# Moving two small coefficient loads, one subtraction of three heads and one step of seven weight blocks in a fused attention and two-layer expert kernel

## The chip, the cores and the metric

The kernel runs on one core of a Trainium2 chip. The metric is the device time of one execution in microseconds (us); lower is better. Five engines work side by side, each through its own queue in order: PE (TensorE, matmuls, with its weight loads shown as PEld), DVE (VectorE), ACT (ScalarE), POOL (GpSimd) and SP (SyncE), which here only issues DMAs. They wait for one another by semaphores.

## The reference

Three stages, all in float32, one after the other:

```python
# attention: 4 batches x 8 heads, 576 positions, 64 channels, causal by blocks of 64
scores = scale * q @ k^T ;  mask where block(i) < block(j) ;  attn = softmax(scores) ;  x = attn @ v
# first layer:  2304 tokens, 512 -> 2048 -> 512
x = leaky_relu(x @ w_in) @ w_out            # slope 0.01
# second layer: 2304 tokens, 512 -> 2048 -> 512
h = x @ w_in ;  P = a0 + a1 h + a2 h^2 + a3 h^3 ;  Q = 1 + |b0||h| + |b1|h^2
out = (P / (Q + 1e-6)) @ w_out
```

The weights arrive as 64-bit numbers and are read as pairs of 32-bit words.

## The kernel before

**Precision.** A matmul operand that must be exact is kept as a rounded high part and the rest, its low part ("hi" and "lo"). A product is then the sum of three matmuls (high by high, and the two crosses), two for the scores of attention. Heads 0 to 7 (`NSF = 8`, `WHOLE = 8`) are computed with plain float32 operands. From head 8 on the heads are "split": `a1(n)` (L249 to L268) makes of q the tiles `QT` and `QM`, of k the tiles `KH` (high part, in both halves) and `KL`, whose upper half is the low part of k, k minus its high part (L266). In the trace these tiles bear the names `split_fq` and `split_fk`. Which engine makes which is told by the letters of `E1` (L124): p is POOL, v DVE, a ACT; the sixth letter is that of L266. The matmuls of scores that read them are L295.

**One head.** The scores go to PSUM (L289 for plain heads, L295 for split ones), DVE takes the row maximum (L301), ACT the exponential (L307), DVE sums and reciprocals (L313, L314), DVE for plain and POOL for split heads scales the probabilities (L317), PE transposes them (L344), ACT and DVE copy them to SBUF (L327 for plain heads; L329, L334, L337 for split ones), PE multiplies by v (L372, L376), and ACT and DVE write the head's result (L383 to L385 for plain heads, L389 to L394 for split ones). After the eighth head of a batch SP saves its last 64 positions (`save_left`, L403). The loop over the 32 heads (L702 to L745) runs these steps for three neighbouring heads at a time, in an order given by strings (`ORDER0`, `ORDER1`, `ORDER`).

**Filling.** When a batch of 8 heads is done, `moe1(b)`, the first layer for its tokens, becomes a filler: a fixed number of its matmuls (L461) is put between the steps of the next batch's heads (`fill`, `FILL`). The 32 units of a batch use the weight blocks one by one; a unit in which the low weights come from memory loads them on SP (L430), up to five units ahead. `gh`, `gl` (L469 to L471) are the activated results, `acc` (L476, L478) their sums.

**Weights.** Each of 64 blocks of weights goes through `convert()` (L157 to L188): SP loads 512 KB into `cs` (L147, three buffers), ACT makes the high words (L165), the low words are made by POOL for the blocks 0 to 15 (L169) and by ACT for all later ones (L171), DVE joins both (L180), ACT rounds (L183), POOL subtracts to get the low part (L184), SP writes it out (L154). Blocks 0 to 31 are the first layer's, the others the second's. How many steps of it stand between the steps of each head is a written list (`due`, `pace`, L675 to L689).

```python
165  nc.scalar.activation(hi.bitcast(F32), hi.bitcast(F32), AF.Prelu, ...)
168  if i < 16:
169      nc.gpsimd.tensor_scalar(lo, lo.bitcast(U32), 0.875 * 2.0 ** -29, 0.4375, ALU.mult, ALU.add)
170  else:
171      nc.scalar.activation(lo, lo.bitcast(U32), AF.Copy, scale=0.875 * 2.0 ** -29, bias=0.4375)
```

**Coefficients.** `cab` (a and b of the second layer, spread over 128 partitions) is loaded on SP near the start, after the first heads' loads (L668, L669); DVE negates a (L670), ACT takes the magnitude of b (L671). They are read only in the second layer (L575 to L589).

**The end.** After the last head the rest of the first layer runs in slices of 24 matmuls (L759 to L774), between which SP loads second-layer weights and the saved positions (L762), and ACT and DVE split them (L764, L765). Then comes the second layer (`moe2`: L563, L617).

**Order.** Only SP's order is the one written in the program (L651). On PE, DVE, ACT and POOL the framework's planner, which sorts ready instructions by priority and by estimated costs, sets the order, so that an instruction can run well ahead of or behind the place where it stands in the code; on the chip each queue then runs in that order.

Of the kernel before, what the change touches and what calls it, by code (L numbers as in the profile page):

```python
# [14 lines left out]
AF = mybir.ActivationFunctionType  # L15
ALU = mybir.AluOpType
# [9 lines left out]
def attention_moe_moe_kernel(  # L26
# [13 lines left out]
    nc = tc.nc  # L40
    P = 128
# [39 lines left out]
    cab = const.tile([P, 6], F32, name="cab")  # L81
    coef = const.tile([P, 6], F32, name="coef")
# [38 lines left out]
    W2H = dram.tile([NF, P, 2 * KD, P], F32, name="w2h")  # L121
    W2L = dram.tile([NF, P, 2 * KD, P], F32, name="w2l")
    NSF = 8
    E1 = "pvpapv"  # L124
    CUTS = [5, 9, 13, 16]
    blocks = []
    for g, c in enumerate(CUTS):
# [16 lines left out]
    def load_block(i):  # L144
        if i < len(blocks):
            stage[i] = cp.tile([P, 512, 2], I32, tag="cs", name="cs", bufs=3)
            nc.sync.dma_start(out=stage[i].rearrange("p (r n) w -> p r (n w)", r=KD), in_=blocks[i][0])  # L147
# [3 lines left out]
    def write_block():  # L151
        if split:
            for d, t in split.pop():
                nc.sync.dma_start(out=d, in_=t)  # L154
            ndone[0] += 1

    def convert():  # L157
        load_block(0)
        load_block(1)
        for i in range(len(blocks) + 1):  # L160
            if i > 0:
                load_block(i + 1)
            if i < len(blocks):
                hi, lo = stage[i][:, :, 1], stage[i][:, :, 0]
                nc.scalar.activation(  # L165
                    hi.bitcast(F32), hi.bitcast(F32), AF.Prelu, scale=2.0 ** -112, alpha=-(2.0 ** 32)
                )
                if i < 16:
                    nc.gpsimd.tensor_scalar(lo, lo.bitcast(U32), 0.875 * 2.0 ** -29, 0.4375, ALU.mult, ALU.add)  # L169
                else:  # L170
                    nc.scalar.activation(lo, lo.bitcast(U32), AF.Copy, scale=0.875 * 2.0 ** -29, bias=0.4375)  # L171
            if i > 0:
                s = stage.pop(i - 1)
                _, (dh, dl), kept = blocks[i - 1]
                hi, lo = s[:, :, 1], s[:, :, 0]
                f = cp.tile([P, KD, P], F32, tag="cl", name="cl", bufs=3)
                wh = dh if kept else cp.tile([P, KD, P], F32R, tag="ch", name="ch", bufs=2)
                hi, lo = (x.rearrange("p (r c) -> p r c", c=P) for x in (hi, lo))
                yield
                nc.vector.scalar_tensor_tensor(  # L180
                    f.bitcast(I32), hi, 3, lo, ALU.logical_shift_left, ALU.bitwise_or
                )
                nc.scalar.copy(wh, f)  # L183
                nc.gpsimd.tensor_tensor(f.bitcast(F32R), f, wh.bitcast(F32), ALU.subtract)  # L184
                write_block()
                split.append(((dh, wh.bitcast(F32)), (dl, f))[kept:])
                yield
        write_block()  # L188

    ndone = [0]  # L190
    conv = convert()

    def cv(n):
# [21 lines left out]
    def split_tiles(n):  # L215
        e, j = n % 2, (2 * n - NSF) % 4
        for d, nm, i in ((QT, "fq", j), (KH, "fk", j), (QM, "fq", j + 1), (KL, "fk", j + 1)):
            d[e] = ap.tile([P, S], F32R, tag=f"{nm}{i % 4}", name=f"split_{nm}{i % 4}")
        for c, d in enumerate((QM, KL)):
            src = plain[(NSF - 1) % 4][c] if n == NSF else d[1 - e].bitcast(F32)  # L220
            cp1("p", d[e][D:P, :], src[D:P, :])
# [19 lines left out]
    def cp1(eng, out, in_, by=1.0):  # L241
        if eng == "a":
            nc.scalar.activation(out, in_, AF.Copy, scale=by)
        elif eng == "v":
            nc.vector.tensor_scalar(out, in_, by, None, ALU.mult)
        else:
            nc.gpsimd.tensor_scalar(out, in_, by, 1.0, ALU.mult, ALU.mult)

    def a1(n):  # L249
        if n < NSF:  # L250
            if n > 0:
                fq = plain[n % 4][0][0:D, :]
                cp1("a", fq, fq, SCALE)
            return
        if n < NSF + 2:
            split_tiles(n)
        e = n % 2
        qs, ks = qk[e][0:D, :], qk[e][D:P, :]
        cp1(E1[0], QT[e][0:D, :], qs, SCALE)
        nc.vector.scalar_tensor_tensor(  # L260
            QT[e][D:P, :], qs, SCALE, QT[e][0:D, :].bitcast(F32), ALU.mult, ALU.subtract
        )
        cp1(E1[2], QM[e][0:D, :], QT[e][0:D, :].bitcast(F32))
        cp1(E1[3], KH[e][D:P, :], ks)
        cp1(E1[4], KH[e][0:D, :], ks)
        (nc.vector if E1[5] == "v" else nc.gpsimd).tensor_tensor(  # L266
            KL[e][0:D, :], ks, KH[e][D:P, :].bitcast(F32), ALU.subtract
        )  # L268

# [218 lines left out]
    def fill(n):  # L488
        if filler[0] is None:
            return  # L490
        for _ in range(n):
            if next(filler[0], 0) == 0:
                filler[0] = None
                return
# [17 lines left out]
    def load_w2_by_part(f, wh, wl):  # L512
        W2[f] = (wh, wl)
        for t, w in ((wh, W2H), (wl, W2L)):
            nc.sync.dma_start(out=t.bitcast(F32), in_=w[f].rearrange("p k c -> p (k c)"))
            yield
# [4 lines left out]
    def x_tiles():  # L521
        return tuple(xp.tile([P, KD, NT1], F32R, tag=nm, name=nm) for nm in ("xh", "xl"))

    def w2_in_x(pair, i):
        x = pair[i].rearrange("p k s -> p (k s)")
        return x[:, 0:1024], x[:, 1024:2048]
# [4 lines left out]
    def load_x2(c):  # L531
        t0, n = chunks[c]
        h = xq[c % 2].tile([P, KD, 512], F32R, tag="x2h", name="x2h")
        l = xq[c % 2].tile([P, KD, 512], F32R, tag="x2l", name="x2l")
        XC[c] = (h, l)
        for t, x in ((h, x2hd), (l, x2ld)):
            nc.sync.dma_start(
                out=t[:, :, 0:n].bitcast(F32), in_=x[:, t0:t0 + n].rearrange("(k p) t -> p k t", p=P)
            )
            yield  # L540
# [110 lines left out]
    with tc.manual_schedule(engines={mybir.EngineType.SP}):  # L651
# [13 lines left out]
            for i in range(5):  # L665
                nc.gpsimd.memset(PB[e][i][:, KEYS[i]:], 0.0)
        nc.vector.memset(cq, 1.0 + EPS_Q)
        nc.sync.dma_start(out=cab[:, 0:4], in_=ca.partition_broadcast(P))  # L668
        nc.sync.dma_start(out=cab[:, 4:6], in_=cb.partition_broadcast(P))  # L669
        nc.vector.tensor_scalar(coef[:, 0:4], cab[:, 0:4], -1.0, None, ALU.mult)  # L670
        nc.scalar.activation(coef[:, 4:6], cab[:, 4:6], AF.Abs)  # L671

        heads = [(b, h) for b in range(B) for h in range(H)]

# [27 lines left out]
        for n, (b, h) in enumerate(heads):  # L702
# [8 lines left out]
            for step, f in zip(steps, fills):  # L711
                if step == "1" and n + 1 < NHD:
                    a1(n + 1)
                elif step == "v":
                    if n >= WHOLE:
                        a1v(n)
                    if n < WHOLE and odd and 0 < p:
                        load_v(p + 1)
                elif step == "4":
                    save_left()  # L720
                    apply(n - 2)
                elif step == "x":
                    a2_part(n, [(0, 4)], (nm, sm))
                elif step == "y":
                    a2_part(n, [(0, 3), (512, 2)], (nm, sm))
                elif step == "z":
                    a2_part(n, [(0, 1), (512, 0)], (nm, sm))
                elif step == "a" and n > 0:
                    if n >= WHOLE and odd and p < NHD // 2 - 1:
                        load_v(p + 1)  # L730
                    a3a(n - 1)
                elif step == "b" and n > 0:
                    a3b(n - 1)
                if step == max("xyz", key=steps.index):
                    a2_norm(n, sm)
                fill(f)
                pace(n, steps.index(step) + 1)
# [21 lines left out]
        for i in range(32):  # L759
            fill(24)  # L760
            if i == 1:
                nc.sync.dma_start(out=X[B][1].bitcast(F32), in_=xld.rearrange("p k b t -> p k (b t)"))  # L762
            elif i == 14:
                nc.scalar.copy(X[B][0], X[B][1].bitcast(F32))  # L764
                nc.vector.tensor_tensor(X[B][1], X[B][1].bitcast(F32), X[B][0].bitcast(F32), ALU.subtract)  # L765
            elif i < 14:
                next(loads, None)
            elif i == 15:
                pair = x_tiles()
                loads = chain(*(load_w2_by_part(NA + 2 + f, *w2_in_x(pair, f)) for f in range(2)))  # L770
                loads = chain(loads, load_x2(0))
                filler[0] = moe1(B) if filler[0] is None else chain(filler[0], moe1(B))
            elif i % 2:
                next(loads, None)  # L774
# [45 lines left out]
```

## Time and profile before

| | |
|---|---|
| median of 3 runs | 1052.02 us (1050.37 to 1052.32) |
| profiled execution, its own time | 1049.87 us |
| its span in the trace | 1048.1 us |
| PE busy | 1000.8 us (95%) |
| DVE, ACT, POOL busy | 741.6, 665.6, 274.0 us (71%, 64%, 26%) |
| mean granted TensorE clock | 0.995 |

Up to about 500 us the 32 heads run, from about 82 us on with the first layer as filler; from there to 645 us the rest of the first layer, then the second. An engine's busy time says how much of the span it worked; the idle time in brackets of a timeline row says how long it stood before that instruction and which instruction of another engine ended the wait.

### The profile page before, as it was taken

The numbers are of one execution on the slowest core, as the hardware profiler recorded it, in microseconds if no ns is written. First come the engines' busy times: TensorE is split into PE (matmuls) and PEld (weight loads), VectorE is DVE, ScalarE is ACT, GpSimd is POOL, SyncE is SP. The second block draws the span as 40 slices with busy tenths as digits, with TensorE's granted clock in tenths as the row PEclk, the third lists the DMA queues.
The fourth block names the chain that finished last, engine by engine and source line by source line (L and its number), as shares of the span: only waits on it lengthen the run. The fifth ranks groups of instructions, "written<-read, shape, count | busy, mean of one in ns | idle before, by whom it ended". The sixth has DMA issues, their size and how long they took to land.

```text
span 1048.1 us, 14697 instructions
## 1 busy us (share of the span) xinstructions
PE 1000.8 (95%) x4968; PEld 826.2 (79%) x4968; DVE 741.6 (71%) x1273; ACT 665.6 (64%) x1364; POOL 274.0 (26%) x329
## 2 busy tenths in 40 slices
PE   7988888898999989999999999999999999999998
PEld 5656767787888877788888899888888888888886
DVE  4896777666777666766332223999888888888875
ACT  5776688776777766675321224876766666676675
POOL 3355656555554545453100101000000000000000
PEclk9999999999999999999999999999999999999999
DMA  8475868668577677564655587802102010110010
GB/s 204 139 208 177 274 191 277 194 211 267 193 229 208 212 249 227 167 221 132 203 192 183 195 286 280 331 1 81 41 1 81 1 40 1 41 41 1 1 41 21
DMA packets 101995, 158.32 MB, mean 151 GB/s; under 512 B 11168, under 2 KB 48032, under 8 KB 101920
## 3 DMA queue, kind: packets, MB, share of 16 engines
q1 hardware_dynamic: 101920, 157.39, 46.8%
q8 instruction: 39, 0.64, 0.2%
q14 instruction: 36, 0.29, 0.1%
HBM read 116.92 MB, written 39.85 MB: 150 GB/s over the span
## 4 chain that ended last, share of the span: by engine, by line
PE 66%; DMA 7%; ACT 5%; DVE 4%; issue 3%; POOL 1%; SPq 1%; ACTq 0%; DVEq 0%; POOLq 0%
PE M L461 23%; PE h L563 19%; PE o L617 19%; DMA cs<-in_moe_w_in_dram 3%; PE T L344 2%; PE T L295 1%; ACT PB L307 1%; PE T L376 1%; DMA cs<-in_moe_w_out_dram 1%; DMA vr<-in_v_dram 1%; ACT pTh L329 1%; ACT cs L165 1%; DMA xld<-vr 1%; DMA w2h<-ch 1%; DVE pTl L337 1%
## 5 line engine op out<-in xcount | busy, mean ns | idle before, releaser
L461 PE MATMUL M<-gh,w1o 128*128 128x512 f32 (+1 forms) x320 | 121.1, 378 | 6.4 <-DVE vr L390 2.5
L461 PE MATMUL M<-gl,w1o 128*128 128x512 f32 (+1 forms) x320 | 121.0, 378 | 0.0
L461 PE MATMUL M<-gh,wl 128*128 128x512 f32 (+1 forms) x320 | 120.5, 377 | 0.0
L575 ACT ACTIVATE ea<-h,coef 128x512 f32<-128x512 f32 (+1 forms) x80 | 51.6, 645 | 92.7 <-PE h L563 92.7
L307 ACT ACTIVATE PB<-T,nm 128x448 f32<-128x448 f32 (+4 forms) x160 | 82.8, 523 | 36.0 <-DVE nm L301 34.0
L469 ACT ACTIVATE gh<-M 128x512 fp32r<-128x512 f32 (+1 forms) x80 | 44.4, 555 | 89.5 <-PE M L461 89.4
L471 DVE TENSOR_TENSOR gl<-M,gh 128x512 fp32r<-128x512 f32 (+1 forms) x80 | 50.4, 632 | 65.5 <-ACT M L470 65.5
L563 PE MATMUL h<-x2h,w2l 128*128 128x512 f32 (+1 forms) x240 | 88.9, 370 | 0.0
L563 PE MATMUL h<-x2h,w2h 128*128 128x512 f32 (+1 forms) x240 | 88.8, 370 | 0.0
L563 PE MATMUL h<-x2l,w2h 128*128 128x512 f32 (+1 forms) x240 | 88.8, 370 | 0.0
L317 POOL TENSOR_SCALAR PB<-PB,sm 128x448 f32<-128x448 f32 (+4 forms) x120 | 71.5, 615 | 53.3 <-DVE sm L314 53.3
L617 PE MATMUL o<-w2h,g2l 128*128 128x512 f32 x216 | 84.7, 392 | 0.0
L617 PE MATMUL o<-w2h,g2h 128*128 128x512 f32 x216 | 84.7, 392 | 0.0
L617 PE MATMUL o<-w2l,g2h 128*128 128x512 f32 x216 | 84.6, 391 | 0.0
L461 PE MATMUL M<-xh,w1i 128*128 128x512 f32 x256 | 76.2, 407 | 5.4 <-DVE vr L390 4.4
L578 DVE SCALAR_TENSOR_TENSOR ea<-eh,coef,ea 128x512 f32<-128x512 f32 (+1 forms) x80 | 55.7, 696 | 34.9 <-ACT eh L576 34.3
L344 PE MATMUL T<-ident,PB 128*128 128x128 f32 x480 | 67.3, 280 | 13.3 <-ACT PB L307 8.8
L301 DVE TENSOR_REDUCE nm<-T 128x1 f32<-128x448 f32 (+4 forms) x160 | 71.7, 479 | 10.7 <-PE T L289 8.7
L344 PEld LDWEIGHTS T<-ident,PB 128*128 128x128 f32 x480 | 55.0, 143 | 28.1 <-ACT PB L307 10.9
L461 PE MATMUL M<-xl,w1i 128*128 128x512 f32 x256 | 72.4, 397 | 3.9 <-DVE xl L384 2.4
L180 DVE SCALAR_TENSOR_TENSOR cl<-cs 128x512 int32<-128x512 int32 x64 | 57.3, 898 | 24.9 <-ACT cs L171 8.3
L461 PEld LDWEIGHTS M<-gh,w1o 128*128 128x128 f32 x320 | 60.7, 190 | 17.6 <-DVE gl L471 2.9
(121 smaller groups left out, 2536.3 us busy)
## 6 DMA issues: line engine op xcount, KB each, us to landing
wl<-w1l SPq DMA_DIRECT2D x160, 256.0 KB, 3.2
cs<-in_moe_w_in_dram SPq DMA_DIRECT2D x32, 512.0 KB, 5.4
cs<-in_moe_w_out_dram SPq DMA_DIRECT2D x32, 512.0 KB, 5.5
w1l<-cl SPq DMA_DIRECT2D x32, 256.0 KB, 4.5
w2h<-ch SPq DMA_DIRECT2D x32, 256.0 KB, 3.6
w2l<-cl SPq DMA_DIRECT2D x32, 256.0 KB, 3.9
w2h<-w2h SPq DMA_DIRECT2D x12, 512.0 KB, 6.5
w2l<-w2l SPq DMA_DIRECT2D x12, 512.0 KB, 7.1
```

The costliest lines, as they stand in the source:

```text
L180: nc.vector.scalar_tensor_tensor(f.bitcast(I32), hi, 3, lo, ALU.logical_shift_left, ALU.bitwise_or)
L301: nc.vector.tensor_reduce(nm[:, i:i + 1], sc, axis=AX.X, op=ALU.max, negate=True)
L307: nc.scalar.activation(PB[e][i][:, 0:ln], sc, AF.Exp, scale=SCALE if n == 0 else 1.0, bias=nm[:, i:i + 1], accum_out=sm[:, i:i + 1])
L317: (nc.vector if n < WHOLE else nc.gpsimd).tensor_scalar(PB[e][i][:, 0:ln], PB[e][i][:, 0:ln], sm[:, i:i + 1], 1.0, ALU.mult, ALU.mult)
L344: nc.tensor.transpose(T[:, c:c + P], PB[e][i][:, kt * P:(kt + 1) * P], ident)
L461: nc.tensor.matmul(T, lhsT=w[:, kk, :], rhs=A[kk][lo], start=(m == 0), stop=(m == 11))
L469: nc.scalar.activation(gh, T, AF.Prelu, alpha=0.01)
L471: nc.vector.tensor_tensor(gl, T, gh.bitcast(F32), ALU.subtract)
L563: nc.tensor.matmul(h[:, 0:n], lhsT=a, rhs=x, start=(kk == 0 and i == 0), stop=(kk == KD - 1 and i == 2))
L575: nc.scalar.activation(a, h, AF.Abs, scale=coef[:, 4:5])
L578: nc.vector.scalar_tensor_tensor(a, h2, coef[:, 5:6], a, ALU.mult, ALU.add)
L617: nc.tensor.matmul(ob[t], lhsT=a, rhs=w, start=(f == 0 and i == 0), stop=(f == NF - 1 and i == 2))
```

## The change

The two loads of coefficients and their two small instructions go from the start to the last group of the first layer: the loads behind the load of the saved positions, the instructions behind the split of these. L266 goes from DVE to POOL for the heads 8, 9 and 10. The low words of the blocks 9 to 15 are made by ACT in place of POOL. The sixth letter of `E1` is not needed any more.

```diff
-    E1 = "pvpapv"
+    E1 = "pvpap"
...
-                if i < 16:
+                if i < 9:
                     nc.gpsimd.tensor_scalar(lo, lo.bitcast(U32), 0.875 * 2.0 ** -29, 0.4375, ALU.mult, ALU.add)
                 else:
                     nc.scalar.activation(lo, lo.bitcast(U32), AF.Copy, scale=0.875 * 2.0 ** -29, bias=0.4375)
...
-        (nc.vector if E1[5] == "v" else nc.gpsimd).tensor_tensor(
+        (nc.gpsimd if n < NSF + 3 else nc.vector).tensor_tensor(
             KL[e][0:D, :], ks, KH[e][D:P, :].bitcast(F32), ALU.subtract
         )
...
         nc.vector.memset(cq, 1.0 + EPS_Q)
-        nc.sync.dma_start(out=cab[:, 0:4], in_=ca.partition_broadcast(P))
-        nc.sync.dma_start(out=cab[:, 4:6], in_=cb.partition_broadcast(P))
-        nc.vector.tensor_scalar(coef[:, 0:4], cab[:, 0:4], -1.0, None, ALU.mult)
-        nc.scalar.activation(coef[:, 4:6], cab[:, 4:6], AF.Abs)
...
             if i == 1:
                 nc.sync.dma_start(out=X[B][1].bitcast(F32), in_=xld.rearrange("p k b t -> p k (b t)"))
+                nc.sync.dma_start(out=cab[:, 0:4], in_=ca.partition_broadcast(P))
+                nc.sync.dma_start(out=cab[:, 4:6], in_=cb.partition_broadcast(P))
             elif i == 14:
                 nc.scalar.copy(X[B][0], X[B][1].bitcast(F32))
                 nc.vector.tensor_tensor(X[B][1], X[B][1].bitcast(F32), X[B][0].bitcast(F32), ALU.subtract)
+                nc.vector.tensor_scalar(coef[:, 0:4], cab[:, 0:4], -1.0, None, ALU.mult)
+                nc.scalar.activation(coef[:, 4:6], cab[:, 4:6], AF.Abs)
```

## Rows read from the trace of the kernel before

**Rows 1.** The page, part 1: busy time, share of the span, instructions.

```profile
PE 1000.8 (95%) x4968; PEld 826.2 (79%) x4968; DVE 741.6 (71%) x1273; ACT 665.6 (64%) x1364; POOL 274.0 (26%) x329
```

**Rows 2.** Windows: busy time and count per engine, TensorE's granted clock, DMA share, GB/s.

```profile
60.00:80.00 20.00, 16.22 (x84) 11.23 (x82) 19.75 (x40) 14.29 (x37) 10.43 (x11) 1.00 0.62 194
80.00:100.00 20.00, 15.74 (x76) 11.95 (x74) 12.64 (x22) 12.46 (x28) 12.14 (x13) 0.91 0.38 115
100.00:120.00 20.00, 17.29 (x92) 14.29 (x91) 13.50 (x23) 14.49 (x32) 11.97 (x14) 1.00 1.02 334
...
500.00:550.00 50.00, 50.00 (x220) 40.67 (x219) 15.06 (x22) 14.58 (x25) 5.16 (x4) 1.00 0.62 206
```

**Rows 3.** Timeline, 12 to 20 us: start, duration, engine, line, idle before and releaser.

```profile
12.06 0.58 SPq L668 DMA_DIRECT2D cab<-in_moe_a_dram  x1
12.69 0.45 SPq L669 DMA_DIRECT2D cab<-in_moe_b_dram  x1
...
14.83 0.17 DVE L670 TENSOR_SCALAR coef<-cab 128x4 f32<-128x4 f32 x1 [1.25 <-DMA cab<-in_moe_a_dram]
...
15.96 0.30 PE L344 MATMUL T<-ident,PB 128*128 128x128 f32 x1 [3.27 <-DVE PB L317]
...
16.18 0.20 ACT L671 ACTIVATE coef<-cab 128x2 f32<-128x2 f32 x1 [2.61 <-DMA cab<-in_moe_b_dram]
...
19.46 0.66 POOL L169 TENSOR_SCALAR cs<-cs 128x512 int32<-128x512 uint32 x1 [13.51 <-DMA cs<-in_moe_w_in_dram]
```

**Rows 4.** L266, L171 and L184 by line: shortest, median and longest in ns.

```profile
L266 DVE TENSOR_TENSOR split_fk<-qk,split_fk x24: 753/755/3704, 61.8 to 460.0; 64x576 fp32r<-64x576 f32 x24
...
L171 ACT ACTIVATE cs<-cs x48: 643/668/738, 116.5 to 472.1; 128x512 int32<-128x512 uint32 x48
...
L184 POOL TENSOR_TENSOR cl<-cl,w1o x16: 1267/1282/1735, 47.8 to 197.3; 128x512 fp32r<-128x512 f32 x16
```

**Rows 5.** Timeline, 61 to 77 us.

```profile
61.76 1.11 DVE L266 TENSOR_TENSOR split_fk<-qk,split_fk 64x576 fp32r<-64x576 f32 x1
...
72.33 3.70 DVE L266 TENSOR_TENSOR split_fk<-qk,split_fk 64x576 fp32r<-64x576 f32 x1
...
74.16 1.27 POOL L184 TENSOR_TENSOR cl<-cl,w1i 128x512 fp32r<-128x512 f32 x1
...
76.63 2.10 PE L376 MATMUL T<-acc,vr 128*128 128x448 f32 x8 [2.02 <-DVE acc L327]
```

**Rows 6.** Timeline, 85 to 92 us.

```profile
85.91 3.49 POOL L317 TENSOR_SCALAR PB<-PB,sm 128x448 f32<-128x448 f32 x5
...
89.49 0.64 POOL L169 TENSOR_SCALAR cs<-cs 128x512 int32<-128x512 uint32 x1
90.16 0.69 DVE L180 SCALAR_TENSOR_TENSOR cl<-cs 128x512 int32<-128x512 int32 x1 [2.57 <-POOL cs L169]
...
91.63 0.50 PE L461 MATMUL M<-xl,w1i 128*128 128x512 f32 x1 [2.45 <-DVE xl L384]
...
91.75 0.61 SPq L403 DMA_DIRECT2D xld<-acc  x1
```

**Rows 7.** Timeline by engine, 112 to 117 us.

```profile
112.98 0.67 POOL L169 TENSOR_SCALAR cs<-cs 128x512 int32<-128x512 uint32 x1
...
113.68 0.69 DVE L180 SCALAR_TENSOR_TENSOR cl<-cs 128x512 int32<-128x512 int32 x1 [2.46 <-POOL cs L169]
...
116.79 0.50 PE L461 MATMUL M<-gh,w1o 128*128 128x512 f32 x1 [1.92 <-DVE gl L471]
```

**Rows 8.** Windows of 4 us: the same columns as in rows 2.

```profile
92.00:96.00 4.00, 4.00 (x14) 3.22 (x13) 1.53 (x3) 2.06 (x6) 1.22 (x1) 0.57 0.66 175
...
104.00:108.00 4.00, 4.00 (x23) 3.51 (x22) 3.90 (x8) 3.16 (x7) 2.72 (x4) 1.00 1.10 345
```

**Rows 9.** Timeline of ACT, 79 to 83 us: the exponentials behind L165 of two blocks.

```profile
79.95 0.64 ACT L307 ACTIVATE PB<-T,nm 128x448 f32<-128x448 f32 x1 [0.24 <-DVE nm L301]
...
82.49 0.42 ACT L307 ACTIVATE PB<-T,nm 128x192 f32<-128x192 f32 x1
```

## The prediction

> **What bounds the kernel now.** I began with the busy times: TensorE works 1000.8 of 1048.1 us [rows 1], so a change that leaves its work alone, as this one does, can win at most the other 47 us, and only where TensorE stands idle or runs at half its clock. The windows say where that is. From 500 us on TensorE is never idle (50.00 of 50.00) and DVE and ACT are 30% busy [rows 2]: nothing moved there counts. Between 60 and 120 us it is idle for 3.78, 4.26 and 2.71 us, 10.75 in all, and in the first of these slices DVE is busy 19.75 of 20 us [rows 2]: there DVE is the bound, and TensorE waits for it. So I read that stretch in the timeline, engine by engine, and the first 20 us, where the coefficients are. Every edit but the move into the last group falls in these two places.
>
> **Part 1, the coefficients leave the start.** DVE stood 1.25 us for the first load and then took 0.17, ACT stood 2.61 and took 0.20; TensorE's transposes stood 3.27 us for the normalised probabilities that DVE makes behind its coefficient instruction [rows 3]. SP's two issues end about 1.1 us after the first begins [rows 3]. At most 1.25 + 0.17 = 1.42 us come free on TensorE's path. But behind it ACT meets the first weight block's first instruction, whose data POOL was still waiting for at 19.46 [rows 3]: that landing moves only as far as SP's issues do, 1.1 us at most, less because the next load waits for the tiles of head 0. Bounds 0 and 1.42; I take 0.5, nearer to the landing, because that wait ends last. In the last group the loads stand behind the load of the saved positions: two SP issues of 0.58 and 0.45, ahead of weight loads that are five units early, and 0.17 + 0.20 us on DVE and ACT while these are 30% busy and TensorE never idle [rows 2, 3]. What hides them is that idle time; if the two instructions were put ahead of their data, DVE and ACT would stand as at the start, at most 2.61 us, with four score banks and five early units of cover. Cost 0.
>
> **Part 2, L266 of heads 8, 9 and 10 goes to GpSimd.** A clean L266 costs DVE 0.755 us (median); of the three that move, head 8's took 1.11 and head 9's 3.70; head 10's I put at no more than head 8's and count it at nothing here [rows 4, 5]. The long one is not work: it began at 72.33 and ended at 76.03, 0.6 us after GpSimd's subtraction that began at 74.16 and took 1.27 had ended [rows 5]. DVE stood for GpSimd's two-input instructions, one behind the other, and TensorE stood 2.02 us at 76.63 for the PSUM copy queued behind L266 on DVE [rows 5]. On GpSimd the operation isn't in the trace. The nearest row is L184, the same subtraction with 512 elements per partition: 1.28 us [rows 4]; at 576 that scales to 1.44. From below 0.755, as on DVE; I take 1.4. So GpSimd gets 3 x 1.4 = 4.2 us more. It gives up 7 low-word steps of 0.64 to 0.67 us [rows 6, 7], 4.6 us, and is busy 10 to 12 of 20 us [rows 2]. The product KL is needed only when the head's scores run, several us later, so its own lateness costs nothing.
> - Head 8: DVE is full, so its 1.11 us come back: 1.1 (0 to 1.1).
> - Head 9: the PSUM copy moves up to 72.3 and TensorE's 2.02 us go. Next late are the sums (L313) and the scaling (L317) of head 7, which came behind L266's end at 76.03 and may now stand for GpSimd in its turn. 2.0 (0 to 3.7).
> - What the new GpSimd instructions hold up on DVE: bounds 0 and 4.2; I take one of the three in full, 1.4, since only at head 9 is GpSimd's queue packed.
>
> **Part 3, the low words of blocks 9 to 15 go to ACT.** Each takes 0.668 us on ACT (median of L171), 7 x 0.668 = 4.7 us in all [rows 4], in a stretch where ACT is busy 14.3, 12.5 and 14.5 of 20 us [rows 2]. What it frees is a queue, not work.
> - Block 12: GpSimd's L169 stood behind the five scalings (85.91, 3.49 us); DVE's join of the words stood 2.57 us for it, with the writing of head 7's result behind it on DVE. For that TensorE stood 2.45 us at 91.63, and SP, whose saving of the last positions (L403) it also holds, issued nothing until 91.75 [rows 6]. ACT has the word ready right behind L165. TensorE's 2.45 us go (0 to 2.45). Head 10's L266, which was ahead of that join, is gone as well.
> - The clock: after that idle time TensorE had a stretch at the lower level, the mean of the slice from 92 is 0.57 [rows 8]. At about 0.5 for 3.4 us it costs 1.7 us. If the idle time goes, I expect the stretch to go, but the low weights, loaded only after L403, then come in second: 0.85 (0 to 1.7).
> - Block 15: the same pattern, DVE stood 2.46 us behind GpSimd and TensorE 1.92 us for `gl` [rows 7]: 1.9 (0 to 2.4).
> - The price on ACT: where an exponential stands right behind L165, it comes 0.668 us later. That is so for blocks 10 and 11, with ACT idle 0.24 us or not at all before it [rows 9]: 2 x 0.668 = 1.35. Bounds 0 and 4.7.
>
> **The sum.** 0.5 + 1.1 + 2.0 - 1.4 + 2.45 + 0.85 + 1.9 - 1.35 = 6.05 us. Against the profiled execution's own 1049.87 us (span 1048.1 and 1.8 around it) that gives 1043.8. This execution was 2.15 us below the median shown, 1052.02; the runs lie 2 us apart. From the median: 1052.02 - 6.05 = 1046.0. A measurement of this kernel can tell about 0.2%, 2.1 us, from no change, so under 1049.9 is faster and over 1054.1 slower.
>
> **Rivals.**
> 1. The wait only changes sides. GpSimd's run at 72.3 gets 1.4 us longer and DVE's sums of head 7 stand for its end at about 76.8 (75.43 + 1.4), where they came behind 76.03: head 9 brings 0, head 8 0.4, block 12 gives back 1.4, and the half-clock stretch stays. 0.5 + 0.4 + 0 + (2.45 - 1.4) + 1.9 - 1.35 = 2.5 us, 1049.5. For it: L266 got no turn in 3.1 us between GpSimd's instructions [rows 5]. Against it: only at head 9 do they stand so close, and the PSUM copy needs no turn. The Trainium skill, SBUF — State Buffer, section "SBUF: two separate sides", says the same of the hardware: DVE and GpSimd share a pair of ports as an exclusive lock, held for a whole instruction, and a DVE instruction with two SBUF inputs stands until GpSimd's is done. The 3.70 us of L266 agree. By that rule alone each of the three would cost DVE up to 1.4 where it saved 0.755. Chance 0.2.
> 2. The transfers take over. From 100 us on the DMA engines are full (share 1.02, and 1.10 in the slice from 104) [rows 2, 8]. If what was won before 92 us is lost waiting for weights, about 1.5 us are left: 1050.5. For it: those slices. Against it: the full stretch begins when SP gets past L403, which comes earlier too. Chance 0.14.
> 3. Slower: ACT becomes the bound between 60 and 120 us. All seven steps lie ahead of something that is waited for, 4.7 us, and the freed waits turn into waits for ACT, of which only the 2.0 us of head 9 stay won: 1052.0 + 4.7 - 2.0 = 1054.7. It decides if of ACT's 18.8 idle us between 60 and 120 [rows 2] hardly any lies where a step is put. Against it: at blocks 12 and 15 ACT was idle, waiting for DVE's join. Chance 0.08.
> 4. Larger: the half-clock stretch early on goes too, with the start's full 1.42 us, and GpSimd holds nothing up: 6.05 + 0.9 + 1.4 + 1.7 = 10 us, 1042.0. Chance 0.08.
>
> That the edits don't do what they say I can exclude: each changes which engine or place a traced line has.
>
> **How the numbers follow.** The forecast has 0.5; its own range is 1043.5 to 1048.5. The planner sorts four engines' queues anew, and where idle time falls decides on half-clock stretches of 1.7 us each, so rivals 1 and 2 have a width of about 1.5 us. Faster takes the forecast, rival 4 and three quarters of rival 1: 0.5 + 0.08 + 0.15 = 0.73. Slower takes rival 3 and 0.03 of the others, 0.11; the rest is 0.16. The range 1042 to 1051 leaves out rival 3, half of rival 4 and some of rival 2.
>
> **What would show it.** Right: no L266 on DVE before about 100 us and none of 3.7 us; DVE's join of block 12 without a wait for GpSimd; L403 on SP some 5 us earlier than 91.75; full clock in the slice where TensorE meets head 7's low part; TensorE's idle time in 60 to 120 us near 5 us instead of 10.75; the second layer starting some 6 us earlier with the same length. Rival 1 shows as an L313 or L180 of several us beside GpSimd's L266; rival 2 as ACT standing for `cs` or TensorE for `wl`; rival 3 as L301's successors late with ACT never idle. I am wrong if the second layer starts less than 2 us earlier.

## The result and the profile after

The changed kernel takes 1041.33 us (median of 4 runs, 1039.60 to 1043.14) against 1051.19 us of the kernel before in the same session (median of 4 runs, 1050.12 to 1052.32): ratio 0.9911, 95% interval 0.9882 to 0.9940. Five more rounds gave 1041.18 us and 0.9909 (0.9888 to 0.9930). It is faster, as forecast, by more than forecast: 1041.3 lies just below the range. The profiled execution took 1041.77 us, its span is 1040.0 us, 8.1 us less than before.

The windows of the changed kernel, columns as in [rows 2]:

```profile
60.00:80.00 20.00, 16.41 (x91) 12.22 (x90) 19.43 (x42) 15.61 (x41) 11.16 (x11) 1.00 0.56 174
80.00:100.00 20.00, 19.26 (x99) 14.86 (x97) 15.04 (x28) 16.87 (x38) 13.49 (x15) 1.00 0.71 233
100.00:120.00 20.00, 18.45 (x100) 15.43 (x99) 14.65 (x26) 18.16 (x39) 11.61 (x13) 1.00 0.96 306
120.00:140.00 20.00, 18.65 (x99) 15.48 (x98) 14.37 (x24) 15.43 (x34) 16.57 (x19) 1.00 0.77 231
```

TensorE's idle time from 60 to 120 us is 3.59 + 0.74 + 1.55 = 5.88 us, where it was 10.75 [rows 2]. The clock is full in all four. The fourth line is one that the prediction had not read. Before, it was this:

```profile
120.00:140.00 20.00, 15.95 (x83) 12.75 (x82) 16.93 (x22) 13.16 (x29) 12.58 (x13) 1.00 0.55 176
```

There TensorE's idle time fell from 4.05 to 1.35 us. Over 60 to 140 us it fell from 14.8 to 7.2, and the half-clock stretch of 92 to 96 us [rows 8] is gone. The timeline of the changed kernel where [rows 5] and [rows 6] were read:

```profile
73.94 1.41 POOL L266 TENSOR_TENSOR split_fk<-qk,split_fk 64x576 fp32r<-64x576 f32 x1
74.58 0.80 DVE L313 TENSOR_SCALAR sm<-sm 128x5 f32<-128x5 f32 x1
75.43 1.27 POOL L184 TENSOR_TENSOR cl<-cl,w1o 128x512 fp32r<-128x512 f32 x1
...
85.86 0.69 DVE L384 TENSOR_TENSOR xl<-T,xh 64x512 fp32r<-64x512 f32 x1 [0.47 <-ACT xh L383]
86.73 0.60 SPq L403 DMA_DIRECT2D xld<-acc  x1
86.73 0.73 DVE L180 SCALAR_TENSOR_TENSOR cl<-cs 128x512 int32<-128x512 int32 x1
```

L266 takes 1.41 us on GpSimd, and the 3.70 us on VectorE are gone; the sums (L313) take 0.80 us beside it, where a clean one takes 0.17. The join of block 12 stands for nothing, and L403 is issued at 86.73 instead of 91.75. Note the order on VectorE: the writing of head 7's result (L384) is now ahead of the join (L180). Before it began at 90.88, behind the join that stands at 90.16 [rows 6].

The second layer starts at 636.88 instead of 645.01, 8.13 us earlier, and is as long as before to 0.05 us. By the same matmuls of the filler, the changed kernel is 10.36 us ahead at 135.00 us of the kernel before; some 2 us of that are lost again by 480 us.

### The profile page after: what moved, and what is told of

Its sections match the earlier page's. It is cut to its first block, busy times and chain, and to the rows that moved or that the text cites. A ratio compares the mean times of both kernels' runs of the same rounds, so it can differ in the third digit from the quotient of the medians.

```text
span 1040.0 us, 14689 instructions
## 1 busy us (share of the span) xinstructions
PE 996.7 (96%) x4968; PEld 822.8 (79%) x4968; DVE 736.7 (71%) x1270; ACT 668.9 (64%) x1371; POOL 271.5 (26%) x325
## 4 chain that ended last, share of the span: by engine, by line
PE 62%; DMA 11%; ACT 9%; DVE 8%; issue 4%; POOL 3%; SPq 2%; ACTq 0%; DVEq 0%; POOLq 0%
PE M L461 20%; PE h L563 19%; PE o L617 19%; DMA cs<-in_moe_w_in_dram 3%; ACT PB L307 3%; DVE nm L301 2%; DMA cs<-in_moe_w_out_dram 2%; DMA xld<-vr 2%; DVE cl L180 1%; ACT cs L165 1%; PE T L344 1%; ACT pTh L329 1%; PE T L376 1%; DMA qk<-in_k_dram 1%; DMA qk<-in_q_dram 1%
## 5 line engine op out<-in xcount | busy, mean ns | idle before, releaser
L317 POOL TENSOR_SCALAR PB<-PB,sm 128x448 f32<-128x448 f32 (+4 forms) x120 | 71.1, 612 | 51.9 <-DVE sm L314 51.9
L180 DVE SCALAR_TENSOR_TENSOR cl<-cs 128x512 int32<-128x512 int32 x64 | 57.0, 892 | 23.0 <-ACT cs L171 9.6
L461 PE MATMUL M<-xh,wl 128*128 128x512 f32 x256 | 73.1, 401 | 0.0
```

The source lines that it names most:

```text
L180: nc.vector.scalar_tensor_tensor(f.bitcast(I32), hi, 3, lo, ALU.logical_shift_left, ALU.bitwise_or)
L317: (nc.vector if n < WHOLE else nc.gpsimd).tensor_scalar(PB[e][i][:, 0:ln], PB[e][i][:, 0:ln], sm[:, i:i + 1], 1.0, ALU.mult, ALU.mult)
L461: nc.tensor.matmul(T, lhsT=w[:, kk, :], rhs=A[kk][lo], start=(m == 0), stop=(m == 11))
```

## The experiments

Each was timed in 5 rounds beside the kernel before, whose medians lay at 1050.0 to 1051.0. "Idle" is TensorE's idle time from 60 to 140 us in that run's one profile (14.8 us before). Single executions of one kernel lie up to 9 us apart, so gains are read from the ratios, and the traces only say where. The second profile of the changed kernel (after_again, 1045.92 us) shows how far a trace can be trusted: it is 9.76 us ahead at 135.00 us, against 10.36 in the first, but its second layer starts only 3.94 us earlier. Up to 140 us the two agree within 0.6 us; what comes behind differs from one execution to the next.

**Which part.**

| kernel | median us | ratio, 95% interval | idle us |
|---|---|---|---|
| p1_coef: part 1 alone | 1050.11 | 0.9998 (0.9982 to 1.0014) | 14.92 |
| p2_kl: part 2 alone | 1048.91 | 0.9994 (0.9979 to 1.0010) | 11.72 |
| p3_lo: part 3 alone | 1042.06 | 0.9921 (0.9900 to 0.9941) | 8.51 |
| p23_no_coef: parts 2 and 3 | 1040.23 | 0.9897 (0.9876 to 0.9919) | 7.25 |
| after_again: all three | 1041.18 | 0.9909 (0.9888 to 0.9930) | 6.76 |

The edits are the hunks of the change's own diff, one part at a time.

> Part 1 alone: only the coefficients leave the start, the rest is the kernel before. Queue theory (the gain was made where GpSimd's queue held up DVE, so by parts 2 and 3; at the start the landing of the first weight block ends last, and the trace of the changed kernel is 0.5 us late at head 4): 0 to 0.5 us slower. Start theory (the half-clock stretch at 17 us goes and what is won there stays): 2 to 3 us faster. Order theory (the planner sorts four queues anew after any edit, and what comes of it is chance): anything from 3 us faster to 3 us slower, with the difference arising after 100 us.

> Part 2 alone: only the low part of k of heads 8 to 10 goes to GpSimd. Queue theory: DVE's 3.7 us stand at head 9 is gone and head 9's first row maximum comes 3 to 3.5 us earlier, as in the changed kernel from head 7 to head 9; the waits at blocks 12 and 15 stay or grow by 1.4 us, since GpSimd's queue is longer; in all 1.5 to 3.5 us faster. Lock theory (GpSimd's new instruction holds DVE up as long as DVE's own did): within 1 us of the kernel before. Order theory: anything within 3 us, arising after 100 us.

> Part 3 alone: only the low words of blocks 9 to 15 go to ScalarE. Queue theory: head 9 is not earlier, but DVE's waits of 2.57 and 2.46 us for GpSimd at blocks 12 and 15 are gone; first-layer matmuls that stand behind them 2.5 to 3.5 us earlier after 97 us and 5 to 7 us earlier after 135 us; in all 4 to 7 us faster. ScalarE theory (4.7 us more on ScalarE come back as waits): 0 to 2 us faster. Order theory: anything within 3 us.

> Parts 2 and 3 together, the coefficients stay at the start. Queue theory: as fast as the whole change or up to 0.5 us faster, 9.9 to 10.4 us under the kernel before. Start theory: 2 to 3 us slower than the whole change, 7 to 8 us under the kernel before. Order theory: parts don't add, more than 2 us from the sum of the two runs with one of them each.

> The changed kernel once more, for its place beside the kernels of this call. 1040 to 1043 us, 8 to 10 us below the kernel before.

Part 3 alone has 0.79% of 1050, 8.3 us (6.2 to 10.5). Parts 1 and 2 alone have nothing that these runs can tell from zero. In the trace of part 2 alone the long L266 is gone and the ninth head (head 8) comes 4.06 us earlier than before, but part of it is given back at block 15, where GpSimd still makes the low word:

```profile
108.07 0.64 POOL L169 TENSOR_SCALAR cs<-cs 128x512 int32<-128x512 uint32 x1
108.74 0.69 DVE L180 SCALAR_TENSOR_TENSOR cl<-cs 128x512 int32<-128x512 int32 x1 [2.83 <-POOL cs L169]
...
111.53 1.47 PE L344 MATMUL T<-ident,PB 128*128 128x128 f32 x8 [2.87 <-POOL cl L184]
...
113.22 0.63 PE L461 MATMUL M<-gh,wl 128*128 128x512 f32 x1
```

TensorE stands 2.87 us, where it stood 1.92 before [rows 7], and then runs at half clock for a stretch (0.63 us for a matmul that takes 0.39 to 0.40 shortly after). By the same matmuls of the filler, part 2 alone is 4.65 us ahead at 111.96 and 2.72 us at 116.79. Its second layer still starts 3.58 us earlier. But this execution (1046.28 us) is the second fastest of twelve, whose median shows no gain; where the others lose it is not shown. The time came as the lock theory said, though not for its reason: the stand at head 9 is gone. In the trace of part 3 alone it is the other way round; VectorE's L266 and TensorE's stand are as before [rows 5]:

```profile
72.53 3.69 DVE L266 TENSOR_TENSOR split_fk<-qk,split_fk 64x576 fp32r<-64x576 f32 x1
76.82 2.10 PE L376 MATMUL T<-acc,vr 128*128 128x448 f32 x8 [2.00 <-DVE acc L327]
```

**Which blocks of part 3.** Base is the kernel before; the three lines are those of lo_9_11, lo_12 and lo_13_15.

```diff
-                if i < 16:
+                if i < 9 or 12 <= i < 16:
+                if i < 16 and i != 12:
+                if i < 13:
```

> The kernel before with only the low words of blocks 9 to 11 made on ScalarE. The run with all seven won 8.3 us. Queue theory (what counts is that GpSimd's low word stands behind the five scalings of a head where DVE's join and SP wait for it, at block 12, and two subtractions in GpSimd's queue that DVE's L260 stands for, at blocks 13 to 15): blocks 9 to 11 bring nothing, 0 to -1 us against before; the join of block 12 still stands over 2 us for GpSimd. Load theory (any step taken from GpSimd helps in proportion): 3/7 of 8.3, -3.6 us. ScalarE theory of the prediction (an exponential right behind costs what the step takes): +1.3 us.

> The kernel before with only the low word of block 12 made on ScalarE. Queue theory: -3.5 to -5 us against before (TensorE's 2.45 us of idle time behind L390 and the half-clock stretch behind it go), SP's L403 about 4 us earlier than 91.75; block 15 still stands over 2 us for GpSimd. Load theory: 1/7 of 8.3, -1.2 us. If the time won at block 12 is given back at block 15, where GpSimd is still behind: 0 to -1.5 us, with TensorE idle over 3 us there.

> The kernel before with only the low words of blocks 13 to 15 made on ScalarE. Queue theory: -3 to -4 us against before (TensorE's 1.9 us at block 15, and its 2.25 us at 133.97 behind DVE's L260 of 3.6 us); the stand at block 12 and the half clock behind it stay, L403 near 91.75. Load theory: 3/7 of 8.3, -3.6 us, so this run alone doesn't tell the two apart; the sum of the three partial runs does (queue theory: about 8 in all, nearly all of it in the last two).

| kernel | median us | ratio, 95% interval | idle us | second layer earlier by |
|---|---|---|---|---|
| lo_9_11 | 1044.19 | 0.9946 (0.9929 to 0.9963) | 9.12 | 3.36 us |
| lo_12 | 1044.54 | 0.9953 (0.9939 to 0.9967) | 9.27 | 6.54 us |
| lo_13_15 | 1048.22 | 0.9986 (0.9972 to 1.0000) | 13.24 | 1.00 us |

The first expectation fell with both its rivals: blocks 9 to 11 bring 5.7 us where the queue theory said none and the load theory 3.6. The second came as the queue theory had it (4.9 us for 3.5 to 5). The third fell too (1.5 us for 3 to 4). The three add up to 12 us, all together to 8.3; the difference of 3.8 us has an interval of about 3.5 us either way, but the traces agree: at the matmul at 135.00 the three are 4.60, 5.11 and 1.61 us ahead, all together 7.86. So blocks 9 to 11 and block 12 remove in part the same things, each by itself. The trace of lo_9_11 says how at block 12:

```profile
87.56 0.69 DVE L384 TENSOR_TENSOR xl<-T,xh 64x512 fp32r<-64x512 f32 x1 [0.45 <-ACT xh L383]
...
88.43 0.61 SPq L403 DMA_DIRECT2D xld<-acc  x1
...
90.28 0.64 POOL L169 TENSOR_SCALAR cs<-cs 128x512 int32<-128x512 uint32 x1
90.96 0.69 DVE L180 SCALAR_TENSOR_TENSOR cl<-cs 128x512 int32<-128x512 int32 x1 [1.77 <-POOL cs L169]
```

GpSimd still makes the low word of block 12 behind its scalings, and VectorE's join still stands 1.77 us for it. But the planner has put L384 ahead of the join, and nothing that TensorE or SP needs is behind it any more. The wait of the join costs TensorE nothing here; what cost was the work queued behind it. In lo_12 the other cure is seen: the join is still ahead of L384, but doesn't wait (1.02 us from 87.67), and TensorE stands 1.14 us for L384 instead of 2.45.

The trace of lo_13_15 keeps the stand at block 12 (2.44 us, half clock behind it) and shows a second one, behind an L260 of 3.64 us. First the same place in the kernel before, then lo_13_15:

```profile
122.79 3.62 DVE L260 SCALAR_TENSOR_TENSOR split_fq<-qk,split_fq 64x576 fp32r<-64x576 f32 x1
...
131.41 1.72 DVE L180 SCALAR_TENSOR_TENSOR cl<-cs 128x512 int32<-128x512 int32 x1 [1.27 <-POOL PB L317]
...
133.97 1.19 PE L461 MATMUL M<-xh,w1i 128*128 128x512 f32 x4 [2.25 <-DVE vr L390]
```

```profile
121.16 3.64 DVE L260 SCALAR_TENSOR_TENSOR split_fq<-qk,split_fq 64x576 fp32r<-64x576 f32 x1
121.64 1.29 POOL L184 TENSOR_TENSOR cl<-cl,w1o 128x512 fp32r<-128x512 f32 x1
122.89 1.29 POOL L184 TENSOR_TENSOR cl<-cl,w1i 128x512 fp32r<-128x512 f32 x1
...
129.78 1.75 DVE L180 SCALAR_TENSOR_TENSOR cl<-cs 128x512 int32<-128x512 int32 x1 [1.26 <-POOL PB L317]
...
131.56 0.75 DVE L390 TENSOR_TENSOR vr<-T,vr 64x576 f32<-64x576 f32 x1
...
132.36 1.19 PE L461 MATMUL M<-xh,w1i 128*128 128x512 f32 x4 [2.24 <-DVE vr L390]
```

L260 doesn't end before GpSimd's two subtractions have ended. Later a join (L180) stands on VectorE right ahead of L390, waits 1.26 us until GpSimd's scalings (L317) have ended, takes 1.75 us, and TensorE stands 2.24 us. In lo_9_11, lo_12, p3_lo and the changed kernel L260 takes 2.43, 1.84, 1.85 and 0.90 us, the joins near L390 wait for nothing, and this stand of TensorE is down to 0.67, 0.42, 0.91 and 0 us. None of the edits touches an instruction there: the low words of these blocks are ScalarE's in the kernel before too. What changed is the order on VectorE and GpSimd.

**Is L260 the cause of that stand?** The two subtractions on VectorE in place of GpSimd, nothing else:

```diff
-                nc.gpsimd.tensor_tensor(f.bitcast(F32R), f, wh.bitcast(F32), ALU.subtract)
+                (nc.vector if i - 1 in (16, 17) else nc.gpsimd).tensor_tensor(f.bitcast(F32R), f, wh.bitcast(F32), ALU.subtract)
```

> The kernel before with two of GpSimd's subtractions (L184 of the blocks 16 and 17, those at 123.27 and 124.51 us, behind which VectorE's L260 took 3.62 us) on VectorE, nothing else moved. Theory that the gain behind 121 us is this stand's: L260 takes about 0.75 us, TensorE's 2.25 us of idle time at 133.97 go, 1 to 2.25 us faster than before, with nothing changed ahead of 120 us. Theory that the bunching is only a sign of a chain that is late for another reason: 0 to +1.5 us (the two subtractions cost VectorE 0.75 us each), TensorE still idle some 2 us near 134.

Measured: 1045.66 us, 0.9950 (0.9931 to 0.9970), 5.2 us faster; the trace:

```profile
124.81 1.15 DVE L184 TENSOR_TENSOR cl<-cl,w1o 128x512 fp32r<-128x512 f32 x1
127.12 0.65 DVE L184 TENSOR_TENSOR cl<-cl,w1i 128x512 fp32r<-128x512 f32 x1
127.80 1.08 DVE L260 SCALAR_TENSOR_TENSOR split_fq<-qk,split_fq 64x576 fp32r<-64x576 f32 x1
130.73 1.60 DVE L180 SCALAR_TENSOR_TENSOR cl<-cs 128x512 int32<-128x512 int32 x2
...
132.36 0.75 DVE L390 TENSOR_TENSOR vr<-T,vr 64x576 f32<-64x576 f32 x1
```

L260 takes 1.08 us, two joins stand ahead of L390 and don't wait, and TensorE's idle time in 120 to 140 us falls from 4.05 to 0.60 us. Between the same two matmuls of the filler (at 120.98 and at 135.00 in the kernel before) this kernel gains 3.07 + 0.62 = 3.69 us. Ahead of the first of them it was 3.07 us late, though nothing is edited there. That the median gains more than the expected 1 to 2.25 us is not explained by this stretch alone.

The run does not show that L260 is the cause, for the joins have moved as well. Two other traces part the two. In p2_kl L260 is short and the stand is there in full:

```profile
121.22 1.83 DVE L260 SCALAR_TENSOR_TENSOR split_fq<-qk,split_fq 64x576 fp32r<-64x576 f32 x1
...
126.98 1.74 DVE L180 SCALAR_TENSOR_TENSOR cl<-cs 128x512 int32<-128x512 int32 x1 [1.27 <-POOL PB L317]
...
129.56 1.19 PE L461 MATMUL M<-xh,w1i 128*128 128x512 f32 x4 [2.23 <-DVE vr L390]
```

In act_none, below, the same instruction takes 0.75 us and TensorE stands 2.62. In the twenty traces, a stand of over 1 us for L390 near this place comes in six, each with one such join right ahead of it, which waits 1.26 to 1.28 us for GpSimd and takes 1.71 to 1.76. Where the joins don't wait, it is 0.91 us at most; in act_twice and act_w448 a join waits 1.22 us, and it is 0.77 and 0.25 us. So the stand hangs on the order of the queues, whatever L260 takes. A shorter L260 gains something of its own: between 120.98 and 133.97 p2_kl wins 1.21 us with the stand still there. Whether a long L260 brings that order about is open.

**The price on ScalarE.** All on the changed kernel: act_twice, act_none, and the three widths (448 stands for each). In all but act_twice the join of blocks 9 to 15 ANDs in place of ORing.

```diff
+                    if i < 16:
+                        nc.scalar.activation(lo, lo.bitcast(U32), AF.Copy, scale=1.0, bias=0.0)
...
-                else:
+                elif i >= 16:
...
-                    nc.scalar.activation(lo, lo.bitcast(U32), AF.Copy, scale=0.875 * 2.0 ** -29, bias=0.4375)
+                    w = 448 if i < 16 else 512; nc.scalar.activation(lo[:, 0:w], lo.bitcast(U32)[:, 0:w], AF.Copy, scale=0.875 * 2.0 ** -29, bias=0.4375)
```

> The changed kernel with a second ScalarE instruction on each low word of blocks 9 to 15, which writes it onto itself: ScalarE has 7 x 0.67 = 4.7 us more work, values unchanged. It doubles the cost that the prediction put at 1.35 us. If ScalarE's added work hides in its idle time: 0 to +1 us against the changed kernel (1041 to 1042.5), the second layer starts within 1 us of 636.9. If it lies on the path as the prediction had it: +1.35 us at least, and +3 to +5 us if all seven do, the second layer starts at 640 or later.

> The changed kernel with no low words at all for the blocks 9 to 15 (the join ANDs the shifted high word with the high word in their place, so the weights of these blocks are other ones): ScalarE has 7 x 0.67 = 4.7 us less work, GpSimd none more. If ScalarE's price is real and doubling it cost 4.8 us because it lies on the path in any case: -1.35 us at least against the changed kernel, up to -4.7. If the single step hides in idle time and only the second one didn't: within 1 us of the changed kernel.

> The changed kernel with the low-word step of blocks 9 to 15 on 448 of the 512 columns (the others stay unconverted, and the join ANDs in place of ORing, so the weights of these blocks are other ones): some 7 x 0.08 = 0.6 us less work on ScalarE, 18 PE and 54 DVE lines of another queue order. Price theory: -0.2 to -0.6 us against the changed kernel, 1040.5 to 1041. Spread theory: anywhere within 3 us of it, also slower.

> The same on 256 of the 512 columns: about half of ScalarE's 4.7 us gone. Price theory: -0.7 to -2.4 us against the changed kernel and faster than with 448 columns. Spread theory: within 3 us of it, in no order with the other widths, and where it is slower the trace shows a stand of VectorE beside GpSimd with TensorE idle behind it.

> The same on 64 of the 512 columns: some 3.5 us of ScalarE's 4.7 gone. Price theory: -1 to -4 us against the changed kernel, the fastest of the three. Spread theory: within 3 us of it, in no order with the other widths.

| kernel | one step, ns | work on ScalarE against the changed kernel | median us | ratio, 95% interval |
|---|---|---|---|---|
| act_twice | 669 + 675 | +4.7 us | 1046.14 | 0.9960 (0.9948 to 0.9972) |
| after_again | 677 | 0 | 1041.18 | 0.9909 (0.9888 to 0.9930) |
| act_w448 | 620 | 7 x 0.057 = -0.4 us | 1044.14 | 0.9939 (0.9923 to 0.9956) |
| act_w256 | 434 | 7 x 0.243 = -1.7 us | 1043.63 | 0.9944 (0.9930 to 0.9958) |
| act_w64 | 253 | 7 x 0.424 = -3.0 us | 1043.10 | 0.9933 (0.9916 to 0.9951) |
| act_none | none | -4.7 us | 1043.85 | 0.9942 (0.9925 to 0.9959) |

For less work the price theory has fallen in its upper size: from -0.4 to -4.7 us the medians lie within 1.1 us, and none is below the changed kernel. The medians of the three widths do fall by 1.0 us in its order, but inside their intervals, and with no step at all the time is above that of the narrowest. From act_w448 to act_none the gain is 0.3 us, with an interval of about 2.5 us either way, so the 1.35 us of the prediction is neither shown nor excluded. All four are some 2.5 to 3.7 us above the changed kernel by the ratios, whose intervals overlap or touch. They share the other join and the other weights, so I can't exclude that these cost something; what two of the traces show (act_none, and with 1.39 us act_w256) is a queue order that brings a stand back. In act_none (its lines are numbered one higher there) it is the stand of L390 again:

```profile
126.36 1.71 DVE L180 SCALAR_TENSOR_TENSOR cl<-cs 128x512 int32<-128x512 int32 x1 [1.28 <-POOL PB L318]
...
128.10 0.75 DVE L391 TENSOR_TENSOR vr<-T,vr 64x576 f32<-64x576 f32 x1
...
128.91 1.19 PE L462 MATMUL M<-xh,w1i 128*128 128x512 f32 x4 [2.62 <-DVE vr L391]
```

For more work the outcome is the other one: doubled, the step costs 5 us. There it lies between the low word and the join that waits for it, and the order is another too; whether ScalarE's slack was used up or the order was worse, one run doesn't tell.

**Further in the same direction.** The bound becomes 5 in p23_lo5 and 0 in the other three; lo0_only has nothing but that on the kernel before, after_lo0 has it on the changed kernel.

```diff
-                if i < 9:
+                if i < 0:
```

> The changed kernel with the coefficients left at the start and the low words on ScalarE from block 5 on (four more, 2.7 us on ScalarE). If taking work from GpSimd's queue keeps paying below block 9, where VectorE was busy 19.75 of 20 us beside it: 1 to 2 us faster than the changed kernel, 1039 or less. If ScalarE is the next limit, as the run with the doubled step says: 1 to 3 us slower than it, 1042 to 1044.

> The changed kernel with the coefficients left at the start and all low words on ScalarE, GpSimd making none. Cover theory: the second head group's DVE-bound stretch (60 to 80 us) gains as it did from block 5 on (TensorE's idle time there 2.4 us in place of 3.6), 1038 to 1040. ScalarE is the limit at the start: heads 2 to 6 come 1 us or more later than in the kernel before, 1041 to 1043.

> The kernel before with all low words on ScalarE and nothing else. The run with parts 2 and 3 and all low words on ScalarE gave 1035.7, 14.5 us below before. If the further gain is the low words' own: 1037 to 1039, 2 us or so short of that run. If it needs GpSimd's queue emptied and the subtraction moved together: 1041 to 1043, no better than the low words of blocks 9 to 15 alone (1042.1), with L266 of 3 us or more on VectorE near 70 us.

> The changed kernel with all low words on ScalarE. If moving the coefficients is worth nothing here as in the other pairs: 1035 to 1037.5. If the start, where ScalarE now has four more steps ahead of 40 us, stands for them (TensorE's transposes stood 1.8 us for ScalarE's copies near 20 us in the changed kernel): 1037.5 to 1040.

| kernel | median us | ratio, 95% interval | idle us |
|---|---|---|---|
| p23_lo5: parts 2 and 3, ScalarE from block 5 | 1039.94 | 0.9904 (0.9883 to 0.9924) | 7.13 |
| p23_lo0: parts 2 and 3, all on ScalarE | 1035.74 | 0.9862 (0.9847 to 0.9877) | 5.75 |
| lo0_only: all on ScalarE, nothing else | 1038.86 | 0.9895 (0.9866 to 0.9924) | 7.47 |
| after_lo0: the changed kernel, all on ScalarE | 1037.74 | 0.9883 (0.9859 to 0.9907) | 7.11 |

p23_lo5 lies between its two expectations and shows no gain over p23_no_coef (0.9904 against 0.9897). p23_lo0 came out faster than either of its own. It has the lowest median of the study, 14.5 us (12.9 to 16.1) below the kernel before. Its windows, against 37.12 us of TensorE in 20 to 60 us before:

```profile
20.00:40.00 20.00, 19.54 (x93) 14.30 (x92) 17.45 (x40) 18.19 (x46) 5.09 (x4) 0.95 0.55 156
40.00:60.00 20.00, 18.87 (x99) 14.05 (x97) 17.27 (x40) 17.18 (x42) 8.92 (x9) 1.00 0.69 219
60.00:80.00 20.00, 17.36 (x91) 12.52 (x91) 19.43 (x43) 18.64 (x49) 11.67 (x14) 1.00 0.63 203
80.00:100.00 20.00, 19.80 (x101) 16.22 (x101) 13.63 (x26) 16.79 (x36) 13.43 (x15) 1.00 0.79 249
```

ScalarE is busy 17 to 18.6 of 20 us from 20 to 80 us and TensorE still stands less than before in every slice. Head 8 comes 6.20 us earlier than before, against 2.91 us in p23_no_coef. lo0_only keeps L266 on VectorE, and there it takes 0.75, 0.74 and 1.21 us for heads 8 to 10: with no low words on GpSimd the planner's order leaves no 3.70 us stand at head 9, so most of part 2's aim is reached without part 2. Its interval overlaps that of p23_lo0, and so does that of after_lo0; which of the three is best stays open.

## Why the prediction was right in direction and too small

**What bounds the kernel: right.** What was won was TensorE's idle time and half clock in 60 to 140 us, most of it behind VectorE's waits; the second layer's length did not change. But I stopped reading at 120 us, and 2.7 of the 7.6 us of idle time that went lay in the next 20.

**Part 3 is the step that failed**: terms 2.45 + 0.85 + 1.9 - 1.35 = 3.85 us, measured 8.3 (6.2 to 10.5) alone. By the same matmuls of the filler in the traces of before and of part 3 alone:
- Block 12 and the clock: 3.3 forecast, 4.3 to 4.9 in the trace (the matmuls at 96.66 and 111.96 come 4.91 and 4.34 us earlier, of which 0.50 was there at 88.59). The whole half-clock stretch went, not half of it. The way was another than I wrote: in that trace, as in the changed kernel's, the join doesn't wait, and L384 has moved ahead of it besides.
- Block 15: 1.9 forecast, 1.0 seen (4.34 to 5.32 us between the matmuls at 111.96 and 120.98). TensorE's stand for `gl` turned into one of 1.37 us for ScalarE's exponential.
- The stretch from L260's 3.62 us to TensorE's stand at 133.97: not in the sum, 2.5 us (5.32 to 7.86 between 120.98 and 135.00). This is the largest single miss. The rows were in the trace, and I read only where I had decided to look. That part 3 would win them could not have been read there: no instruction of that stretch is edited, and the stand shrank because the planner's order changed. These 2.5 us came by luck, not by anything that the prediction had foreseen.
- The price on ScalarE: 1.35 forecast, not seen apart: 4.3 us less work (act_none against act_w448) brought 0.3 us, about 2.5 either way. The three gains above, 4.34 + 0.98 + 2.54 = 7.86 us at 135.00, already contain whatever it cost.

**Part 2: right in mechanism, 1.7 us forecast, 1.8 us from p3_lo to p23_no_coef (1042.06 to 1040.23), whose intervals overlap.** In the changed kernel L313 lost 0.6 us beside GpSimd, and the scaling behind it (L317) took 2.79 us where it had taken 1.56: 1.9 us held up, 1.4 forecast. Alone it gave 0.6 us (-1.1 to 2.2). Its one trace shows 1.9 us lost at block 15, where GpSimd's low word still stands ahead of the join, and none at block 12 (TensorE's stand there is 1.03 us instead of 2.45). That part 2 needs part 3 would fit this, but the trace keeps 3.58 us that the median doesn't show, so it stays open.

**Part 1: 0.5 forecast, 0.2 us measured (-1.5 to 1.9), which can't tell 0.5 from nothing.** The bound of 1.42 us was met at its place: TensorE's stand fell from 3.27 [rows 3] to 1.82 us. It was given back within 10 us, as the timeline of the changed kernel shows:

```profile
13.80 0.30 PE L344 MATMUL T<-ident,PB 128*128 128x128 f32 x1 [1.82 <-DVE PB L317]
...
20.03 1.56 PE L289 MATMUL T<-fk,fq 128*128 128x448 f32 x4 [1.78 <-ACT acc L327]
...
22.33 4.05 DVE L317 TENSOR_SCALAR PB<-PB,sm 128x448 f32<-128x448 f32 x5
22.57 0.74 POOL L169 TENSOR_SCALAR cs<-cs 128x512 int32<-128x512 uint32 x1 [1.82 <-DMA cs<-in_moe_w_in_dram]
23.39 2.58 POOL L184 TENSOR_TENSOR cl<-cl,w1i 128x512 fp32r<-128x512 f32 x2
```

TensorE waits for ScalarE instead, and L317 runs into GpSimd's subtractions: 4.05 us for five, where it took 2.63 before. Head 4 is 0.49 us later than before. In the trace of part 1 alone heads 4 to 8 are 0.13 to 0.44 us earlier.

**The rivals.** 1 (the wait changes sides) did not come as written: in the changed kernel VectorE lost 1.9 us at L313 and L317, and block 12 gave nothing back. In the trace of part 2 alone a stand grew elsewhere, at block 15. 2 (transfers) did not come: the slice from 100 us has a DMA share of 0.96, and TensorE is idle less in it. 3 (ScalarE) did not come with one step per block, and not even with all 16 blocks on it. 4 (1042.0) had the size, but its reasons, the start and GpSimd holding nothing up, are not the ones that paid. Of what I said would show it, all came: no L266 on VectorE before 99.03 us, the join of block 12 without a wait, L403 5.02 us earlier, full clock, 5.88 us of idle time for 5 forecast, the second layer 8.1 us earlier for 6.

## What to carry to other kernels

A wait costs what is queued behind it: before pricing one, list what follows it on its engine, and what a planner that sorts queues anew might put there. When one pattern of row explains a loss, search the whole trace for it, and for every stand of the bottleneck engine, before adding up. And test such a pattern against the traces that have it without the loss: here the long L260 stood beside a stand of TensorE that also came without it. An edit worth 1 us can't be told here: the intervals are 1.5 to 3 us either way, and each edit changes the queue order as well, which brought stands of over 2 us and took them away. Measure groups of edits that meet in one queue together: the three sets of blocks gave 12 us in sum and 8 together.

## What the hardware showed that was not expected

- A VectorE instruction with two SBUF inputs mostly got no turn between two GpSimd subtractions that follow closely: L266 took 3.69 to 3.71 us and L260 3.62 to 3.64 us beside two of 1.25 to 1.29 us each, against 0.75 us clean; beside one of 1.31 us L260 took 1.85 us in p3_lo. In each of these rows it ended 0.6 us after the last of the subtractions. In the long ones a scaling of GpSimd (L247) was running when it began, which [rows 5] doesn't show:

```profile
72.28 0.67 POOL L247 TENSOR_SCALAR split_fq<-split_fq 64x576 fp32r<-64x576 f32 x1
72.92 1.28 POOL L184 TENSOR_TENSOR cl<-cl,w1o 128x512 fp32r<-128x512 f32 x1
```

  Once it did get a turn, in act_w448, where it began beside the first subtraction: it took 1.55 us, ended 0.6 us after that one, and the second took 1.80 us.

```profile
117.64 1.29 POOL L184 TENSOR_TENSOR cl<-cl,w1o 128x512 fp32r<-128x512 f32 x1
117.98 1.55 DVE L260 SCALAR_TENSOR_TENSOR split_fq<-qk,split_fq 64x576 fp32r<-64x576 f32 x1
118.88 1.80 POOL L184 TENSOR_TENSOR cl<-cl,w1i 128x512 fp32r<-128x512 f32 x1
```

  The Trainium skill, SBUF — State Buffer, section "SBUF: two separate sides", has the lock for one instruction's length. These rows agree with it, and show that the length of a whole run can count.
- Stands of TensorE of 1.8 to 4.3 us were followed by a stretch at the lower of its two levels in many places (0.57 mean in [rows 8], 0.63 us a matmul in part 2 alone), so that the stand of [rows 6] cost some 1.7 us more than its own length. Not after each: that of 2.62 us in act_none and those of 1.4 to 1.5 us between 110 and 145 us in the changed kernel were not followed by one. Nor does the length decide alone: behind the same stand of 2.0 us near 76.7 us the clock fell in the traces of lo_9_11 and lo_12, and not in those of the kernel before and p3_lo.
- The room on ScalarE: in lo0_only it took over 16 x 0.67 = 10.7 us of work, in slices from 20 to 120 us where it had been busy 12.5 to 15.7 of 20 us, and the kernel became 11.0 us (8.0 to 14.1) faster.
